# The first x rows loaded as two partition halves from two queues, and two small gate loads moved to GpSimd's queue

## The chip, the cores and the metric

The kernel runs on one core of a Trainium2 chip. The core has a matrix engine (TensorE, PE in the profile), VectorE (DVE), ScalarE (ACT), GpSimd (POOL), SyncE (SP, which here only issues DMAs) and 16 DMA engines that all queues share. Times are microseconds of device time for one execution; lower is better.

## The reference

The kernel mixes two spectral filters of the same input with a gate per row:

```python
def filt(x, w_r, w_i):                       # x: (1, 2048, 1024) bf16
    X = rfft2(x.astype(float32), axes=(-2, -1))
    X = X * (w_r + 1j * w_i)                  # w: (2048, 513)
    return irfft2(X, s=(2048, 1024), axes=(-2, -1)).astype(bfloat16)

g = sigmoid((A_x * gate_w).sum(-1, keepdims=True))   # gate_w: (1024,)
out = g * filt(A_x, A_w_r, A_w_i) + (1 - g) * filt(A_x, B_w_r, B_w_i)
```

## The kernel before

The Fourier transforms are done as matrix products with constant matrices. x is laid out as 64 x 2 groups on 128 partitions, with 16 "rows" j of 1024 elements in each partition (`x` is a view of the tile `XR`); the host has reordered the columns, so that sums and differences of column blocks give the even and odd frequencies.

Stage f1 multiplies each row j by the small matrix `F1` (tile `f` in the profile): 16 matmuls of 64 x 128 by 256 for one row, eight on partitions 0 to 63 and eight on 64 to 127 by turns (line 293); or, for rows that were folded beforehand, 16 matmuls of half the width (line 284). `xfold` (lines 267 and 268) is that fold: a sum and a difference on VectorE. Two halves of PSUM are then evicted to `y`, one by ScalarE and one by VectorE (helper `evac`, lines 250 and 252). Then follow f2 (line 347, products with `FD`), f3 (366, with `WF`), the product with the filter weights `cmul` (387), the way back i1 (414, with `WI`), a write of the result to DRAM scratch `sc` and its fetch in another order, and i2, i3 and the last sums.

The order of the work on each engine is written out by hand in the string `ORDER`, and every engine works through its instructions in that order. It begins `r0:AV V3 r1:AV r2:AV f3:AV r4:AV`: f1 of row 0, the fold of row 3 on VectorE, f1 of rows 1 and 2, f1 of the folded row 3, f1 of row 4. TensorE is kept busy from the start by eight matmuls on a zeroed tile `warm` (line 168). PSUM has eight banks; every stage takes two.

Loads. ScalarE's queue issues `F1` (line 170), `gws` (172, the gate vector, 128 partitions of 8 bf16) and `sg` (174, 128 partitions of one float). SP's queue issues x (line 180): rows 0 and 1 one by one (256 KB each), then pairs of rows (512 KB each), then rows 14 and 15 one by one; behind them `FD`, `WF`, the filter weights and the rest in one long stream. The framework gives the loads of SP and ScalarE eight completion semaphores in turn, so that the issue of one load waits until the load eight places before it has landed. GpSimd clears `gwz` (line 232) and later copies single columns of the weights (341) and issues the small copy `zt` (319).

VectorE turns `gws` into `gwz` with seven small instructions (lines 238 to 246) that stand ahead of all its evictions in its order. `gwz` is read at about 26 us, when the gate's sums are made (line 313); `sg` is read by the sigmoid (line 332) at about 40 us.

Of the kernel before, what the change touches and what calls it, by code (L numbers as in the profile page):

```python
# [141 lines left out]
def gated_mix(ctx, tc, x_in, we_in, wo_in, gw_in, out):  # L142
    nc = tc.nc
    cn = make_constants()
    dr = {n: nc.inline_tensor(a, name=f"cst_{n.lower()}").ap() for n, a in cn.items()}
# [23 lines left out]
    F1 = const.tile([P, 192], BF16, name="f1")  # L169
    nc.scalar.dma_start(F1[:], dr["F1"])  # L170
    gws = const.tile([P, 8], BF16, name="gws")
    nc.scalar.dma_start(gws[:], gw_in)
    sg = const.tile([P, 1], F32, name="sg")
    nc.scalar.dma_start(sg[:], dr["SG"])

    XR = big.tile([P, 16 * 1024], BF16, name="xr")
    RO = big.tile([P, 16 * 1024], BF16, name="ro")
    x = XR[:].rearrange("p (j d) -> p j d", j=16)
    for j0, n in ((0, 1), (1, 1)) + tuple((j, 2) for j in range(2, 14, 2)) + ((14, 1), (15, 1)):
        nc.sync.dma_start(x[:, j0:j0 + n, :], x_in[j0 // 2, :, j0 % 2:j0 % 2 + n, :])  # L180
    FD = const.tile([P, 2, 2, 2, 256], BF16, name="fd")
    IG = const.tile([P, 2, 4, 256], BF16, name="ig")
    WF = const.tile([P, NT, 3, 64], BF16, name="wf")
# [400 lines left out]
```

## Time and profile before

| | |
|---|---|
| median of 3 runs | 112.07 us (111.82 to 112.93) |
| the profiled execution | 112.45 us, of which the span of the core's instructions is 110.7 us |
| busy, share of the span | PE 92%, DVE 84%, ACT 83%, POOL 6% |
| HBM read, written | 24.23 MB, 12.58 MB |
| f1 of row 0 starts on PE | 4.71 us |
| f1 of row 2 starts on PE | 8.01 us, after 0.27 us of waiting for x |
| gate chain on DVE | 5.03 to 5.89 us |

Times inside an execution count from the start of the span. A timeline line gives start, duration, engine, source line, operation, tile written <- tiles read, count, and in brackets the idle time before it and what ended it. A line of the chain of waits gives start, duration and what the time went to. In the table by stretches the columns are the stretch, its length, busy time and number of instructions of PE, PE weight loads, DVE, ACT and POOL, the granted TensorE clock, the DMA engines' busy share and GB/s. A line of the DMA issues gives tile <- source, queue, operation, count, KB of each, and the median us from issue to landing.

### The profile page before, as it was taken

To read this page: it belongs to the slowest core of one execution; us is meant where nothing else is said; L and a number is where in the kernel's file an instruction comes from. 1 tells how busy PE (TensorE), PEld (TensorE's weight loads), DVE (VectorE), ACT (ScalarE), POOL (GpSimd) and SP (SyncE) were. 2 spreads that over 40 slices of the span, in tenths; PEclk is the share of its full clock that TensorE was granted. 3 is DMA by queue.
4 is the path that set the end of the run, shared out by engine and by line. 5 is a ranking of instruction groups with operands and counts; after the bars stand their busy time and mean duration, and the time that the engine had idled before them with its cause. 6 is when DMAs were issued, how large, how long until landed. Compare 5 with 4: busy or idle time off the path is not lost.

```text
span 110.7 us, 3975 instructions
## 1 busy us (share of the span) xinstructions
PE 101.7 (92%) x1669; PEld 65.7 (59%) x1672; DVE 93.4 (84%) x140; ACT 92.3 (83%) x179; POOL 6.7 (6%) x14
## 2 busy tenths in 40 slices
PE   5999997999999999999999999999999979999720
PEld 2369996765656565655555655455697866664400
DVE  0149987897859999999999999999989998678970
ACT  2346786698988999999999998999899998999730
POOL 1000000240520025000000000000000000000000
PEclk9999999999999999999999999999999999999997
DMA  3899999999999999979554999999997999995594
GB/s 111 208 342 418 407 410 405 415 421 390 407 410 397 400 394 392 402 282 294 196 190 136 278 282 403 395 381 354 374 314 206 367 349 394 419 412 235 240 378 191
DMA packets 17650, 37.07 MB, mean 335 GB/s; under 512 B 1884, under 2 KB 10208, under 8 KB 17632
## 3 DMA queue, kind: packets, MB, share of 16 engines
q1 hardware_dynamic: 17168, 36.76, 90.1%
q8 instruction: 13, 0.21, 0.8%
q10 hardware_dynamic: 432, 0.05, 0.3%
q14 instruction: 5, 0.04, 0.1%
q0 software_dynamic: 32, 0.00, 0.0%
HBM read 24.23 MB, written 12.58 MB: 333 GB/s over the span
## 4 chain that ended last, share of the span: by engine, by line
PE 66%; DMA 16%; DVE 6%; ACT 4%; issue 3%; SPq 1%; DVEq 0%; ACTq 0%
PE pt L414 27%; PE pt L347 12%; PE pt L366 6%; DMA ro<-sc 6%; DMA xr<-in_x_dram 6%; PE pt L296 4%; PE pt L293 4%; DMA sc<-rl 4%; PE pt L477 4%; PE pt L444 2%; DVE ot L508 2%; PE pt L459 2%; PE pt L313 2%; ACT V L250 1%; PE pt L284 1%
## 5 line engine op out<-in xcount | busy, mean ns | idle before, releaser
L414 PE MATMUL pt<-p,wi 64*64 64x512 bf16 x512 | 32.6, 379 | 0.1
L250 ACT CAST rl<-pt 128x512 bf16<-128x512 f32 x42 | 24.9, 660 | 1.9 <-PE pt L414 1.6
L387 DVE TENSOR_TENSOR p<-X,ro 128x4096 bf16<-128x4096 bf16 x11 | 25.2, 2295 | 1.2 <-ACT X L250 0.9
L414 PEld LDWEIGHTS <-wi 64*64 64x64 bf16 x512 | 13.3, 106 | 10.4 <-issue 1.5
L250 ACT CAST X<-pt 128x512 bf16<-128x512 f32 x29 | 16.7, 649 | 1.8 <-PE pt L366 1.6
L250 ACT CAST T<-pt 128x512 bf16<-128x512 f32 x30 | 17.3, 671 | 0.0
L347 PE MATMUL pt<-fd,y 128*128 128x256 bf16 x128 | 16.6, 274 | 0.0
L250 ACT CAST V<-pt 128x512 bf16<-128x512 f32 x30 | 16.5, 624 | 0.1
L252 DVE CAST rl<-pt 128x512 bf16<-128x512 f32 x22 | 14.7, 686 | 1.5 <-PE pt L414 1.4
L250 ACT CAST y<-pt 128x512 bf16<-128x512 f32 x17 | 9.7, 606 | 6.6 <-PE pt L293 5.3
L347 PEld LDWEIGHTS <-y 128*128 128x128 bf16 x128 | 11.3, 98 | 5.7 <-issue 4.3
L508 DVE TENSOR_TENSOR ot<-wo,od 128x1024 bf16<-128x1024 bf16 (+1 forms) x18 | 10.9, 631 | 1.3 <-DMA ro<-sc 0.8
L459 PE MATMUL pt<-ig,V 128*128 128x256 bf16 x88 | 11.6, 273 | 0.2
L252 DVE CAST y<-pt 128x512 bf16<-128x512 f32 x15 | 9.9, 686 | 1.4 <-PE pt L293 0.8
L366 PE MATMUL pt<-T,wf 64*64 64x512 bf16 (+2 forms) x192 | 9.8, 306 | 0.0
L387 DVE TENSOR_TENSOR p<-X,wo 128x4096 bf16<-128x4096 bf16 x4 | 9.1, 2284 | 0.0
L459 PEld LDWEIGHTS <-V 128*128 128x128 bf16 x88 | 7.6, 98 | 2.1 <-ACT V L250 1.0
L250 ACT CAST cs<-pt 128x512 bf16<-128x512 f32 x14 | 8.5, 654 | 0.0
L293 PE MATMUL pt<-f,xr 64*128 64x256 bf16 x112 | 7.9, 297 | 0.3 <-DMA xr<-in_x_dram 0.3
L366 PEld LDWEIGHTS <-wf 64*64 64x64 bf16 x192 | 5.3, 106 | 4.4 <-issue 0.4
L293 PEld LDWEIGHTS <-xr 64*128 64x128 bf16 x112 | 5.7, 104 | 2.5 <-issue 0.8
L250 ACT CAST od<-pt 128x512 bf16<-128x512 f32 x10 | 6.0, 624 | 1.4 <-PE pt L477 1.2
(51 smaller groups left out, 101.9 us busy)
## 6 DMA issues: line engine op xcount, KB each, us to landing
sc<-rl SPq DMA_DIRECT2D x16, 512.0 KB, 5.5
xr<-sc SPq DMA_DIRECT2D x8, 512.0 KB, 6.2
ro<-sc SPq DMA_DIRECT2D x8, 512.0 KB, 8.1
ro<-in_we_dram SPq DMA_DIRECT2D x7, 516.0 KB, 8.6
out_dram<-ot SPq DMA_DIRECT2D x7, 512.0 KB, 3.4
xr<-in_x_dram SPq DMA_DIRECT2D x6, 512.0 KB, 8.1
wo<-in_wo_dram SPq DMA_DIRECT2D x4, 512.0 KB, 7.5
ro<-in_wo_dram SPq DMA_DIRECT2D x4, 512.0 KB, 8.5
```

The lines of the kernel that those rows point to most:

```text
L250: nc.scalar.copy(out=out, in_=in_)
L252: nc.vector.tensor_copy(out=out, in_=in_)
L293: nc.tensor.matmul(pv[h][:, :, c, :, :].rearrange("p a e k -> p e a k"), lhsT=xs(j0, h, q), rhs=fs(h, 0, *st), start=(q == 0), stop=(q == 3))
L296: nc.tensor.matmul(pv[h][:, a, c, :, :], lhsT=xs(items[a][0], h, q), rhs=fs(h, items[a][1] * st[1], st[0]), start=(q == 0), stop=(q == 3))
L313: nc.tensor.matmul(ps[32 * j:32 * j + 32, :], lhsT=gwz[:, k, :], rhs=yf[:, 512 * j:512 * j + 512], start=(k == 0), stop=(k == 7))
L347: nc.tensor.matmul(ps[tt][:, e * 256:e * 256 + 256], lhsT=y[par][:, c, e, t].rearrange("p b s k -> p (b s k)"), rhs=FD[:, par, c, e, :], s ...
L366: nc.tensor.matmul(ps[tt][ho, dst:dst + ln], lhsT=WF[hp(j), 2 * u + tt, w, :], rhs=T[hp(j), tt, src:src + ln], start=(k == 0), stop=(k == 2))
L387: nc.vector.tensor_tensor(po, xo, wo, ALU.mult)
L414: nc.tensor.matmul(ps[tt][hp(j), :], lhsT=WI[hin, 2 * u + tt, w, :], rhs=p[hin, q, tt, a::2, o:o + 256], start=(k == 0), stop=(k == 3))
L459: nc.tensor.matmul(po, lhsT=V[:, s, 2 * r + c, :], rhs=IG[:, par, 2 * r + c, :], start=(c == 0), stop=(c == 1))
L477: nc.tensor.matmul(ps[s][:].rearrange("p (a d) -> p a d", a=2), lhsT=V[:, s, 2 * r + c, :], rhs=rhs, start=(r + c == 0), stop=(r + c == 2))
L508: nc.vector.tensor_tensor(o4[:, k, h] if not isinstance(od, list) else o4[:, k.start, h], x, y_, op)
```

## The change

Rows 0 to 3 (three loads: row 0, row 1, rows 2 and 3) are each loaded as two DMAs: partitions 0 to 63 from SP's queue, partitions 64 to 127 from ScalarE's queue. All later x loads stay whole on SP's queue. `gws` and `sg` are issued from GpSimd's queue instead of ScalarE's. On each engine the order of the other instructions is the same as before: SP still issues ten x loads, ScalarE issues F1 and the three halves ahead of its table load and first activation, and GpSimd issues gws and sg ahead of the clear of `gwz`. Line numbers after this place are two higher than before.

```diff
     F1 = const.tile([P, 192], BF16, name="f1")
     nc.scalar.dma_start(F1[:], dr["F1"])
     gws = const.tile([P, 8], BF16, name="gws")
-    nc.scalar.dma_start(gws[:], gw_in)
+    nc.gpsimd.dma_start(gws[:], gw_in)
     sg = const.tile([P, 1], F32, name="sg")
-    nc.scalar.dma_start(sg[:], dr["SG"])
+    nc.gpsimd.dma_start(sg[:], dr["SG"])
...
     for j0, n in ((0, 1), (1, 1)) + tuple((j, 2) for j in range(2, 14, 2)) + ((14, 1), (15, 1)):
-        nc.sync.dma_start(x[:, j0:j0 + n, :], x_in[j0 // 2, :, j0 % 2:j0 % 2 + n, :])
+
+        for q, h in ((nc.sync, slice(0, 64)), (nc.scalar, slice(64, 128))) if j0 < 4 else ((nc.sync, slice(0, 128)),):
+            q.dma_start(x[h, j0:j0 + n, :], x_in[j0 // 2, h, j0 % 2:j0 % 2 + n, :])
```

## The prediction

> **What bounds the kernel now.** I read the page first (TensorE busy for 92% of the span, VectorE 84%, ScalarE 83%), then the chain of waits in order of time, because the change touches the first microseconds only.
>
> ```profile
> 1.64 6.32 DMA xr<-in_x_dram
> ...
> 8.01 1.05 PE pt L293 x16
> 9.05 0.45 PE pt L284 x16
> 9.50 2.62 PE pt L293 x48
> ```
>
> The chain starts with the third x load (rows 2 and 3), which lands at 7.96 us and releases the f1 of row 2 (L293). From there the chain is nearly all TensorE as far as 78 us. What the change is worth is therefore what it does to TensorE's place at about 9 us. I next read the timeline of TensorE and of VectorE for that stretch.
>
> ```profile
> 1.18 3.60 PE L168 MATMUL pt<-warm 128*128 128x512 bf16 x8 [1.18 <-DVE warm L165]
> 4.71 3.03 PE L293 MATMUL pt<-f,xr 64*128 64x256 bf16 x32
> 8.01 1.05 PE L293 MATMUL pt<-f,xr 64*128 64x256 bf16 x16 [0.27 <-DMA xr<-in_x_dram]
> ```
> ```profile
> 5.03 0.17 DVE L238 TENSOR_SCALAR gh<-gws 128x8 f32<-128x8 bf16 x1 [3.91 <-DMA gws<-in_gw_dram]
> ...
> 5.73 0.16 DVE L246 TENSOR_TENSOR gwz<-gh 128x2 bf16<-128x2 f32 x1
> 6.66 0.69 DVE L252 CAST y<-pt 128x512 bf16<-128x512 f32 x1 [0.77 <-PE pt L293]
> 7.98 0.43 DVE L267 TENSOR_TENSOR xf<-xr 128x512 bf16<-128x512 bf16 x1 [0.63 <-DMA xr<-in_x_dram]
> 8.32 0.42 DVE L268 TENSOR_TENSOR xf<-xr 128x512 bf16<-128x512 bf16 x1
> ```
>
> TensorE waits only 0.27 us for rows 2 and 3. VectorE works in program order: the gate chain (7 instructions, 5.03 to 5.89), the eviction of row 0, the fold of row 3, and only then can f3 (L284, first matmul 8.89) start. Last, the stretches of the DMA traffic and the DMA issues:
>
> ```profile
> 2.00:3.00 1.00, 1.00 (x4) 0.44 (x3) 0.00 (x0) 0.88 (x1) 0.00 (x0) 1.00 0.97 347
> 3.00:4.00 1.00, 1.00 (x4) 0.32 (x3) 0.00 (x0) 0.60 (x2) 0.00 (x0) 1.00 0.94 209
> 4.00:5.00 1.00, 1.00 (x6) 0.24 (x6) 0.00 (x0) 0.00 (x0) 0.00 (x0) 1.00 0.92 162
> 5.00:6.00 1.00, 1.00 (x14) 0.67 (x12) 0.79 (x7) 0.00 (x0) 0.00 (x0) 1.00 0.68 217
> ...
> 8.00:9.00 1.00, 0.99 (x20) 0.90 (x22) 1.00 (x3) 0.38 (x1) 0.00 (x0) 1.00 1.02 418
> ```
> ```profile
> f<-cst_f ACTq DMA_DIRECT2D x1, 48.0 KB, 2.7
> gws<-in_gw_dram ACTq DMA_DIRECT2D x1, 2.0 KB, 3.9
> sg<-cst_sg ACTq DMA_DIRECT2D x1, 0.5 KB, 6.6
> ...
> zt<-zs POOLq DMA_DIRECT2D x1, 4.0 KB, 5.6
> ```
>
> The last column of the stretches is GB/s. The rate falls from 347 to 162 and returns to 418 only after 8 us, just while gws (landing at 5.0) and sg (1.63 + 6.6 = 8.2) trickle in. Issue and landing of the x loads tell the same: row 0 at 3.7, row 1 at 4.8, rows 2-3 at 7.96, rows 4-5 at 2.10 + 7.1 = 9.2, rows 6-7 at 10.5. From 7.96 on 512 KB take 1.25 us; between row 1 and rows 2-3 they took 3.2 us. The two tiny loads go with some 1.9 us of lost transfer.
>
> **The change, part by part.**
>
> *ScalarE's queue.* It issues four loads instead of three, at 0.36 to 0.49 us each: 0.5 us more, so the table load and its activation (1.28 and 0.20 us) end near 4.1. Its first eviction was at 6.63, so 2.5 us of slack hide this. Without that slack it would cost its 0.5 us.
>
> *SP's queue.* Ten issues as before. In before, SP stood 1.9 us waiting for sg before it could issue the last x load (a DMA waits for the one eight places before it). That wait goes. It is worth nothing: the transfers ran at 381 to 418 GB/s while SP waited, so the queue had work. The same holds for all later loads, which keep their relative order; if the stream runs up to a microsecond earlier, no TensorE wait of the chain between 9 and 79 us is for a load from the inputs.
>
> *Row 0 and TensorE's start.* TensorE needs both halves and F1. The second half now stands behind F1 in ScalarE's queue, and SP meanwhile moves row 1's first half and part of row 2-3. Best case it lands as before, 3.7; worst, as row 1 did, 4.8, plus the 0.4 us that ScalarE's issue lies behind SP's: 5.2. The warm-up matmuls cover it until 4.78. I take 4.7: nothing, with up to 0.4 us as the upper end.
>
> *Rows 2-3.* Loads that stood in the two queues at the same time have landed together by their number of rows, whatever the rows' size: F1 and row 0 (128 rows each) at 3.4 and 3.7, gws and row 1 at 5.0 and 4.8, sg and rows 2-3 at 8.2 and 7.96. If that is the rule, SP's 64 + 64 + 64 + 128 rows to the end of rows 4-5 run beside ScalarE's 128 (F1) + 64 + 64 + 64, and the second half of rows 2-3 ends with rows 4-5. The lower bound is the same 1.6 MB without tiny packets: begun at about 1.9, at 390 GB/s (between the 347 and 418 above), 6.0 us. The upper is today's landing of rows 4-5, 9.2. The tiny loads still exist, and part of their packets falls into this stretch: I take 8.2, near the row for rows 2-3 and two thirds of the way to the upper end. That is 0.2 us later than now; the bounds are -0.27 us (TensorE is busy until 7.74 anyway) and +1.2 us.
>
> *gws on GpSimd's queue.* The only row of that queue is zt: 0.77 us of issue, 5.6 us to landing. On ScalarE's queue gws took 3.9. GpSimd is free at 0.72. Bounds: 0.72 + 3.9 = 4.6 and 0.72 + 5.6 + 2.4 = 8.7, where 2.4 is what 128 tiny rows took beside a full queue (gws landed 1.6 us after F1 and sg 3.2 us after gws; the mean). Nearest is zt's own 5.6, and I add a third of the 2.4, 0.8, for twice its 64 rows and a second busy queue: landing 7.1. From there on VectorE's order gives: chain 0.86, gap 0.04, eviction 0.69, gap 0.03, fold to first f3 matmul 0.91, together 2.5 us. f3 starts at 9.6 instead of 8.89, so +0.7 us. Up to a landing of 6.4 it costs nothing; at 8.7 it costs 2.3. The delay of rows 2-3 lies under the same wait (f3 would start at 9.1 by it), so the larger counts. VectorE is then busy with one gap of 0.13 us until 16.4, TensorE without one until 18.46, and neither has room to make it up.
>
> *The rest of GpSimd.* The gwz clear (0.31 us) stands behind both issues and ends near 0.72 + 2 x 0.77 + 0.31 = 2.6; it is needed by the fourth instruction of the gate chain, after gws. sg is read at 40 us. Nothing for both.
>
> *Sum.* 0.7 us for the gate chain, 0 for all else. The profiled execution took 112.45 us with a span of 110.7 (1.75 around it); it lies 0.38 above the median of the runs, 112.07. So 113.15 for an execution like that one, 112.8 against the median. Under 1.1 us, 1%, a difference can hardly be told from none here; the forecast is inside that.
>
> **The rivals.**
>
> *A. gws comes much later.* GpSimd's first DMA of the kernel adds most of the 2.4 us: landing 8.1 to 8.7, +1.7 to +2.3 us, time 113.8 to 114.4. It decides from a landing of 7.5 on (+1.1). For: zt's 5.6, which had few packets. Against: zt was issued while VectorE ran a 2.3 us product (27.90 to 30.21), and GpSimd's next instruction beside it took 0.54 us where the one after it took 0.25; at 0.7 us VectorE is idle, so zt's row may be too slow a guide. The Trainium skill (SBUF — State Buffer, Who interferes with whom) says that such a product, with two inputs in SBUF, holds up only GpSimd instructions that read SBUF; by that rule, zt's 5.6 would not come from the product. No run here shows it. Chance 0.24.
>
> *B. The halves move slowly.* Two loads of 64 partitions each don't reach the rate of one over 128, or the tiny packets all fall into the stretch again: rows 2-3's second half lands with rows 4-5 at 9.2 or later. At half of 418 GB/s the 1.0 MB of rows 0 to 3 alone take 5.0 us, to 6.9, and half of the 1.9 us lost to the tiny loads, with part of rows 4-5 (512 KB, 1.25 us) between, make 9.1. TensorE starts row 2 at 9.2, +1.2 us, 113.3. For: equal numbers of rows in the two queues. Against: no row of before shows a half load; the one load over 64 partitions, zt, says nothing of rates. The Trainium skill (SBUF — State Buffer, "Can I just issue two DMAs to hit both halves?") speaks for this: two concurrent loads, at partition 0 and at partition 64, gave it only 6% over a single one, and it wants one load over all 128. No run here shows halves yet. Chance 0.18.
>
> *C. TensorE's full rate comes later.* The matmuls of L293 that start between 4.7 and 6.9 follow each other by about 0.10 us (22 of them), those after 9.5 by 0.055 (48 in 2.62 us). If row 0 is late enough to break the unbroken work since 1.18, the step to the full rate may come later; each 2 us at the low rate cost 0.9 us. With a step 2.7 us late: +1.2, 113.3. Nothing in this trace shows such a break. Chance 0.06.
>
> *D. It does what it says.* gws lands by 6.2 and rows 2-3 by 7.7: the 0.27 us wait goes, 111.8. For: the halves are moved at 390 GB/s if the tiny packets come late. Against: then gws is late too. Chance 0.12.
>
> **How the numbers follow.** Forecast 0.35, A 0.24, B 0.18, C 0.06, D 0.12; 0.05 stay for a gain over 1% that I can't derive, since 0.27 us is all that TensorE waits for these loads. Faster 0.05; within 1% 0.35 + 0.12 = 0.47; slower 0.24 + 0.18 + 0.06 = 0.48. The range goes from just under D, 111.7, into A, 114.2; the forecast's own is 112.1 to 113.1.
>
> **What would show it.** gws's issue on GpSimd's queue and its landing (7.1); the VectorE gate chain starting there; f3's first matmul (9.6); rows 2-3's second half (8.2); the GB/s between 3 and 6 us, which should rise if the tiny loads were the cause. Wrong if TensorE's first unbroken stretch starts before 7.9 or after 9.2, or if a wait elsewhere than in the first 10 us changes by over 0.5 us.

## The result, and the profile after

The changed kernel is slower: a ratio of 1.0129 to the kernel before (95% interval 1.0100 to 1.0157), 20 runs of each, medians 114.0 and 112.91 us. The ratio leaves out executions over 1.5% above the fastest of their kernel (7 of 20 before, 1 of 20 after); over all of them the medians differ by 1.09 us, 0.97%. The profiled execution took 113.27 us, its span 111.5. The load that TensorE waits for is now the second half of rows 2 and 3, on ScalarE's queue. First the chain of waits of the changed kernel, then its TensorE timeline and its VectorE timeline:

```profile
2.43 6.40 DMA xr<-in_x_dram
```
```profile
4.70 2.36 PE L295 MATMUL pt<-f,xr 64*128 64x256 bf16 x33
8.88 1.04 PE L295 MATMUL pt<-f,xr 64*128 64x256 bf16 x15 [1.81 <-DMA xr<-in_x_dram]
```
```profile
4.70 0.17 DVE L240 TENSOR_SCALAR gh<-gws 128x8 f32<-128x8 bf16 x1 [3.58 <-DMA gws<-in_gw_dram]
...
6.16 0.69 DVE L254 CAST y<-pt 128x512 bf16<-128x512 f32 x1 [0.60 <-PE pt L295]
8.92 0.42 DVE L269 TENSOR_TENSOR xf<-xr 128x512 bf16<-128x512 bf16 x1 [2.08 <-DMA xr<-in_x_dram]
```

The load is issued at 2.43 and lands at 8.83, where the whole load of before landed at 7.96. TensorE waits 1.81 us instead of 0.27 and starts row 2 at 8.88 instead of 8.01. (The start tells more than the wait: in before_again TensorE waited 0.79 us, more than the 0.1 to 0.5 that was expected of it, because rows 0 and 1 were done earlier, and still started row 2 at 8.02.) The gate chain on VectorE starts earlier than before, 4.70 against 5.03: gws came in good time. The fold of row 3 waits for the x load, not for the gate. The DMA issues and the stretches (the last column is GB/s):

```profile
xr<-in_x_dram ACTq DMA_DIRECT2D x1, 256.0 KB, 6.4
...
gws<-in_gw_dram POOLq DMA_DIRECT2D x1, 2.0 KB, 3.4
sg<-cst_sg POOLq DMA_DIRECT2D x1, 0.5 KB, 3.3
```
```profile
5.00:6.00 1.00, 1.00 (x18) 0.81 (x16) 0.52 (x6) 0.00 (x0) 0.00 (x0) 1.00 1.21 217
6.00:7.00 1.00, 1.00 (x19) 0.69 (x15) 0.69 (x1) 0.60 (x2) 0.00 (x0) 1.00 0.84 233
7.00:8.00 1.00, 0.07 (x1) 0.00 (x0) 0.00 (x0) 0.58 (x1) 0.00 (x0) 1.00 0.98 274
8.00:9.00 1.00, 0.12 (x3) 0.12 (x5) 0.08 (x1) 0.00 (x0) 0.00 (x0) 1.00 1.02 356
```

gws and sg both land by 5.3, and yet the rate stays under 280 GB/s until 8 us: worse than before (340 and 381 from 6 to 8). Between 7.1 and 8.9 us TensorE does nothing.

To separate the change from what varies anyway, I split the span at two marks: the first matmul of f2 (L347, L349 in the changed kernel) and the end of i1 (L414, L416). Each row is one profiled execution.

| kernel | profiled, us | rows 2-3 complete | f2 starts | f2 to end of i1 | end of i1 to end of span |
|---|---|---|---|---|---|
| before | 112.45 | 7.96 | 17.43 | 60.95 | 32.3 |
| before_again | 113.72 | 7.97 | 17.44 | 60.95 | 33.6 |
| after | 113.27 | 8.83 | 18.56 | 60.95 | 32.0 |
| after_again | 114.31 | 8.45 | 18.36 | 60.95 | 33.2 |

The middle is the same to a hundredth; what is lost before f2 is lost for good. The change costs 1.12 and 0.92 us there, about 0.9% of the time. The last stretch varies by over 1 us in either kernel, mostly by how long TensorE waits for the fetch of `sc` (before_again and after_again, the waits after 80 us):

```profile
PE pt L444 <- DMA ro<-sc: 1.8, 2, 1.3
```
```profile
PE pt L446 <- DMA ro<-sc: 0.9, 2, 0.6
```

after had no such wait, before 0.6 us. So the start of f2 is the sharper measure of this change; whole times that differ by some 0.5% may differ by this wait alone. What is over 0.9% in the ratio of 1.0129 isn't shown to come from the change.

In the changed kernel's two profiles, row 2 starts 0.87 and 0.49 us late. The rest (0.25 and 0.43) comes from 15.3 us on, where TensorE waits for rows 12 and 13. In after:

```profile
PEld L298 <- DMA xr<-in_x_dram: 0.2, 1, 0.2
```

That load landed at 15.65 and 15.36, some 2.5 us behind the one ahead of it, in place of 1.24 before (14.22). A 16 KB instruction fetch of 0.98 us begins at 13.3 to 13.6 us in both. Before has one of 0.95 us at 12.79 and no such gap, and the cause stays open.

### The profile page after: what moved, and what is told of

Its sections match the earlier page's. It is cut to its first block, busy times and chain, and to the rows that moved or that the text cites. A ratio compares the mean times of both kernels' runs of the same rounds, so it can differ in the third digit from the quotient of the medians.

```text
span 111.5 us, 3983 instructions
## 1 busy us (share of the span) xinstructions
PE 101.2 (91%) x1672; PEld 65.6 (59%) x1672; DVE 93.2 (84%) x140; ACT 92.1 (83%) x179; POOL 5.9 (5%) x16
## 4 chain that ended last, share of the span: by engine, by line
PE 73%; ACT 6%; DVE 6%; DMA 6%; issue 3%; ACTq 1%; DVEq 0%
PE pt L416 27%; PE pt L349 12%; PE pt L461 8%; PE pt L368 6%; DMA xr<-in_x_dram 6%; PE pt L446 5%; PE pt L298 4%; PE pt L295 4%; PE pt L479 3%; ACT V L252 3%; DVE ot L510 2%; ACT cs L252 2%; PE pt L315 2%; PE pt L286 1%; DVE p L389 1%
## 5 line engine op out<-in xcount | busy, mean ns | idle before, releaser
L416 PE MATMUL pt<-p,wi 64*64 64x512 bf16 x512 | 32.6, 379 | 0.0
L416 PEld LDWEIGHTS <-wi 64*64 64x64 bf16 x512 | 13.3, 106 | 10.4 <-issue 1.5
L252 ACT CAST V<-pt 128x512 bf16<-128x512 f32 x30 | 17.4, 682 | 0.1
L349 PE MATMUL pt<-fd,y 128*128 128x256 bf16 x128 | 16.6, 274 | 0.0
L349 PEld LDWEIGHTS <-y 128*128 128x128 bf16 x128 | 11.3, 98 | 5.7 <-issue 4.3
L295 PE MATMUL pt<-f,xr 64*128 64x256 bf16 x112 | 7.4, 278 | 1.8 <-DMA xr<-in_x_dram 1.8
L252 ACT CAST cs<-pt 128x512 bf16<-128x512 f32 x14 | 9.0, 713 | 0.0
L252 ACT CAST od<-pt 128x512 bf16<-128x512 f32 x10 | 6.5, 741 | 0.9 <-PE pt L479 0.9
```

The lines of the kernel that those rows point to most:

```text
L252: nc.scalar.copy(out=out, in_=in_)
L295: nc.tensor.matmul(pv[h][:, :, c, :, :].rearrange("p a e k -> p e a k"), lhsT=xs(j0, h, q), rhs=fs(h, 0, *st), start=(q == 0), stop=(q == 3))
L349: nc.tensor.matmul(ps[tt][:, e * 256:e * 256 + 256], lhsT=y[par][:, c, e, t].rearrange("p b s k -> p (b s k)"), rhs=FD[:, par, c, e, :], s ...
L416: nc.tensor.matmul(ps[tt][hp(j), :], lhsT=WI[hin, 2 * u + tt, w, :], rhs=p[hin, q, tt, a::2, o:o + 256], start=(k == 0), stop=(k == 3))
```

## The experiments

The stated theories: H, the halves cost; G, the two loads on GpSimd's queue cost. Under H, a half load is slow in itself (H1, later P), or it is the sharing of two queues (H2), or the number of issues (Q).

### One part alone

move_only has the two `nc.gpsimd.dma_start` lines of the change and loads x as before. halves_only has the halves and leaves `gws` and `sg` on `nc.scalar`.

> x is loaded whole from SP's queue as before; only gws and sg go to GpSimd's queue. Theory H (the halves are what costs: rows 2-3 arrive late because they are split over two queues): rows 2-3 land at 6.0 to 8.0, TensorE starts row 2 before 8.1, time 0.995 to 1.002 of before. Theory G (gws and sg on GpSimd's queue disturb the x loads): rows 2-3 land after 8.5 and the time is 1.008 or more of before. If the tiny packets on ScalarE's queue were what lowered the transfer rate between 3 and 6 us, that rate is over 300 GB/s here and rows 2-3 land before 7; if not, it stays near 200 GB/s and they land near 8.

> gws and sg stay on ScalarE's queue ahead of the second halves, the halves are as in the changed kernel. Theory H: as slow as the changed kernel or slower, since the second halves also stand behind two tiny loads: rows 2-3's second half lands at 9 to 10.5, time 1.01 to 1.03 of before. Theory G: rows 2-3 land near 8, time within 0.5% of before.

move_only: ratio 1.0011 (0.9968 to 1.0055), rows 2-3 at 8.15, f2 at 17.82. G falls as the cause of the loss: rows 2-3 land before 8.5, and the time can't be told from that of before. Nothing at all is more than the runs show, though. By the mark this one profile is 0.39 us late, 0.19 of it at row 2 (8.20), and late_even_odd below, which begins with the same loads, 0.27 (17.71). So part of the changed kernel's 0.92 to 1.12 us may go with the two moved loads. The rate between 3 and 7 us still falls, though gws's and sg's packets are out of ScalarE's queue; they land at 6.10 and 7.23, so they are still under way in that stretch:

```profile
3.00:4.00 1.00, 1.00 (x4) 0.32 (x3) 0.00 (x0) 0.00 (x0) 0.00 (x0) 1.00 0.88 225
...
5.00:6.00 1.00, 1.00 (x14) 0.67 (x12) 0.00 (x0) 0.00 (x0) 0.00 (x0) 1.00 0.85 213
6.00:7.00 1.00, 1.00 (x12) 0.70 (x10) 0.80 (x8) 0.37 (x1) 0.00 (x0) 1.00 0.85 283
```

halves_only: ratio 1.0133 (1.0054 to 1.0212); its executions spread from 113.7 to 118.2, median 116.27, and the ratio rests on the three shortest (113.74, 114.06, 115.38). The profile is of a long one (117.05). In it the second half of row 0 landed at 7.00 and that of rows 2-3 at 10.46. TensorE stood 1.95 us in the middle of row 0, and fell back to its low rate at about 8.4 us, ahead of the next wait. Its timeline, the stretches (the granted clock is third from the right), and the matmuls of line 295 from 10.5 to 16 us (minimum, median, maximum in ns):

```profile
7.04 2.64 PE L295 MATMUL pt<-f,xr 64*128 64x256 bf16 x32 [1.95 <-DMA xr<-in_x_dram]
10.50 1.88 PE L295 MATMUL pt<-f,xr 64*128 64x256 bf16 x15 [0.82 <-DMA xr<-in_x_dram]
```
```profile
8.00:9.00 1.00, 0.94 (x14) 0.71 (x14) 0.69 (x1) 0.59 (x1) 0.00 (x0) 0.78 1.02 234
9.00:10.00 1.00, 0.68 (x8) 0.15 (x2) 0.00 (x0) 0.49 (x1) 0.00 (x0) 0.50 0.98 258
```
```profile
L295 PE MATMUL pt<-f,xr x50: 269/417/418, 10.5 to 15.9; 64*128 64x256 bf16 x50
```

Half of these took 417 ns or more, where 269 is the full rate. The clock stays at 0.50 until about 15.3 us. f2 starts at 22.25, 4.8 us late, and the three executions that the ratio rests on are only 1.1 to 2.7 us longer than the median of before beside them (112.66), so they can't have lost as much. The full rate is not late here, as the prediction's rival C had it, but lost again, and in another kernel: the changed kernel's two profiles have 1.00 throughout the stretches to 16 us. The Trainium skill (TensorE: Matmul & The Clock Gate, Part 1) says that the clock is halved after an idle window of about 3.4 us; the one wait ahead of the fall, 1.95 us, is shorter. The measurement decides: the clock fell here with no longer wait between the first matmul and the fall. What brought it down, no experiment tried.

### Where the loads stand, and in which shape

```diff
 # halves_one_queue: the second half on SP's queue too
-... (nc.scalar, slice(64, 128))) if j0 < 4
+... (nc.sync, slice(64, 128))) if j0 < 4
 # whole_two_queues: rows 0 to 3 whole, one load for each row
+q = nc.scalar if j0 in (1, 3) else nc.sync
+q.dma_start(x[:, j0:j0 + n, :], x_in[j0 // 2, :, j0 % 2:j0 % 2 + n, :])
 # even_odd: halves of even and odd partitions
+(nc.sync, slice(0, 128, 2)), (nc.scalar, slice(1, 128, 2))
 # halves_rows23: "if j0 == 2";  halves_rows01: "if j0 < 2"
 # single_rows: move_only with rows 2 and 3 as two whole loads from SP's queue
 # f1_on_gpsimd: the changed kernel with F1 issued by nc.gpsimd
 # even_odd_f1: even_odd with F1 issued by nc.gpsimd
 # late_halves, late_even_odd: move_only, rows 8-9 and 10-11 as halves, all from SP's queue
```

> Both halves of each load are issued from SP's queue, one after the other; gws and sg on GpSimd's queue. Theory H1 (half loads are slow in themselves, whichever queue): rows 2-3 land at 8.8 or later, time 1.01 or more of before. Theory H2 (the second halves are late because rows 4-5 on SP's queue share the engines with them): here rows 4-5 stand behind both halves, rows 2-3 land where move_only has them plus the 1.2 us of three more issues at most, time below 1.006 of before.

> Rows 0 to 3 are loaded whole (128 partitions), one load for each row: 0 and 2 from SP's queue, 1 and 3 from ScalarE's; gws and sg on GpSimd's queue. Theory H1 (half loads are slow in themselves): rows 2 and 3 land at 8 or before, time within 0.5% of before. Theory H2 (sharing with rows 4-5 makes ScalarE's last load late): row 3 lands with rows 4-5 near 9, but row 2 earlier, TensorE starts row 2 before 8 and waits for the folded row 3 (its first matmul after 9.5 instead of 8.9), time 1.005 to 1.012 of before.

> As the changed kernel, but the two halves are the even and the odd partitions instead of 0 to 63 and 64 to 127: the same loads, rows, bytes, queues and issues. Theory P (a half load over 64 neighbouring partitions runs at half the rate, since these are only half of the ways into the memory; halves_one_queue had 256 KB in 1.25 us where whole loads have 512 KB): even and odd partitions each reach all of them, rows 2-3 land by 8.0, TensorE waits less than 0.5 us for row 2, time 0.997 to 1.005 of before. Theory Q (twice the number of loads, with their issue times and the sharing of two queues, is what costs): rows 2-3 land at 8.8 as in the changed kernel, time 1.009 to 1.016 of before.

> Only rows 2 and 3 are loaded as halves 0 to 63 and 64 to 127 from the two queues; rows 0 and 1 stay whole on SP's queue, gws and sg on GpSimd's. ScalarE's queue has only F1 and the second half. Theory P: the second half lands early (5 to 6.5), beside rows 0 and 1, and the first half, then alone, takes 1.25 us instead of 0.6: rows 2-3 complete at 7.5 to 8.5, time 0.997 to 1.006 of before. Theory Q: two more issues and sharing only: the same or better, 7 to 8. If rows 2-3 land after 8.8 the cost of halves lies in rows 2-3 themselves, and not in the four halves of rows 0 and 1 that stand ahead of them in the changed kernel.

> All x whole from SP's queue, rows 2 and 3 as two loads of 256 KB instead of one of 512 KB; gws and sg on GpSimd's queue. TensorE needs only row 2 first. All theories: row 2 lands at 6 to 7, the wait for it (0.27 us before) goes, row 3 at 8.0 to 8.2 holds the fold and f3 (first matmul 9.0), so at most 0.2 us is gained: time 0.996 to 1.002 of before.

> The changed kernel itself, for a second profiled execution and its times beside the other three on one chip. Expected: 1.010 to 1.016 of before; TensorE waits 1.0 to 2.0 us for rows 2 and 3. If the wait is much the same and the time is 114.0 to 114.5 instead of the 113.3 of the first profiled execution, the rest of the difference lies elsewhere in the span, and the two profiles tell where.

> The changed kernel, with F1's load moved from the head of ScalarE's queue to the head of GpSimd's, so that the two halves of each load stand at the same place of their queues. Theory H2 (ScalarE's halves are late because F1's 128 rows stand ahead of them and rows 4-5 on SP's queue take their turns meanwhile): the second half of rows 2-3 lands within 0.7 us of the first and both by 7.8, TensorE's wait for row 2 falls under 0.6 us, TensorE's f2 of unit 0 starts before 18.2 (18.56 and 18.36 in the changed kernel's two profiles, 17.43 before), time 1.000 to 1.007 of before. Theory Q (twice as many issues, each longer, is what costs, whatever the order): rows 2-3 land at 8.3 or later, f2 at 18.2 or later, time 1.009 or more. F1 may itself be late (landing over 4.8): then the first matmul starts later by as much, and f2 by no more than 0.5 us.

> Rows 0 and 1 as halves from the two queues, rows 2 and 3 whole from SP's queue behind its two first halves; gws and sg on GpSimd's queue. Theory H2: rows 2-3 stand on SP's queue, ahead of rows 4-5, and land by 8.2; the second half of row 1 by 6.2; TensorE's f2 of unit 0 starts before 18.0, time 0.998 to 1.006 of before. Theory Q: the two longer issues at the head of each queue delay everything behind them by 0.4 us or more: rows 2-3 at 8.4 or later, f2 after 18.0, time 1.004 to 1.010.

> The kernel before, for a second profiled execution. Expected of all theories: f2 of unit 0 starts at 17.2 to 17.9, TensorE waits 0.1 to 0.5 us for row 2. It tells how far the stretch from the end of i1 to the end of the span (32.3 us in the first profile, 32.0 and 33.2 in the changed kernel's two) varies without any change.

| kernel | ratio (95% interval) | rows 2-3: first, second part | f2 starts |
|---|---|---|---|
| halves_one_queue | 1.0131 (1.0060 to 1.0202) | 7.15, 8.40 | 18.83 |
| whole_two_queues | 1.0051 (1.0008 to 1.0094) | 6.05, 8.67 (rows 2, 3) | 17.95 |
| even_odd | 1.0042 (1.0000 to 1.0083) | 6.29, 9.14 | 18.68 |
| halves_rows23 | 1.0045 (0.9993 to 1.0097) | 7.26, 6.84 | 17.77 |
| halves_rows01 | 0.9986 (0.9950 to 1.0023) | 6.83 (whole) | 17.28 |
| single_rows | 0.9994 (0.9926 to 1.0062) | 6.90, 7.52 (rows 2, 3) | 17.30 |
| after_again | 1.0146 (1.0041 to 1.0250) | 6.81, 8.45 | 18.36 |
| f1_on_gpsimd | 1.0108 (1.0055 to 1.0160) | 9.44, 9.12 | 18.90 |

(after_again, halves_one_queue and f1_on_gpsimd have four executions each, the others ten.) Few theories met all their numbers: halves_one_queue landed at 8.40 where H1 had 8.8, whole_two_queues started f3 at 9.18 where H2 had 9.5, even_odd met P's ratio but Q's landing, halves_rows23 was complete at 7.26, ahead of P's 7.5 and within Q's 7 to 8, and f1_on_gpsimd met all of Q's, which halves_rows01 (6.83, where Q had 8.4) speaks against.

Three things follow. First, the place in the two queues matters. Counting rows of loads from the head of each queue, some loads that stand at the same count land at nearly the same time: in whole_two_queues rows 1 and 2 (256 rows) at 6.23 and 6.05, row 3 and rows 4-5 (384) at 8.67 and 8.13; in halves_rows01 row 1's second half and rows 2-3 (256) at 6.37 and 6.83; in the changed kernel the second half of rows 2-3 and rows 4-5 (320) at 8.83 and 9.43. It is no rule, though. In the changed kernel itself the second half of row 1 (256) lands at 5.62, ahead of the first half of rows 2-3 (192) at 6.74; in halves_rows23 the second half of rows 2-3 (192) lands at 6.84, long after row 1 (256) at 4.76; in halves_only 448 rows are in at 7.00 in one queue and at 11.42 in the other. With rows 2-3 whole and on SP's queue ahead of rows 4-5, as in halves_rows01, TensorE does not wait for them at all:

```profile
4.70 3.53 PE L295 MATMUL pt<-f,xr 64*128 64x256 bf16 x47
```

Second, the place isn't the whole. f1_on_gpsimd gives both halves the same place, they do land together, and late, at 9.1 to 9.4, and halves_one_queue has no sharing and is as slow as the changed kernel. H2 alone falls. Third, the parts don't add: halves of rows 0 and 1 alone cost nothing, halves of rows 2 and 3 alone 0.3 us at f2, no more than move_only without any (with rows 2-3 complete at 7.26, but 0.58 us of waiting for rows 12 and 13), both 0.9 to 1.1. even_odd stayed unclear: rows 2-3 as late as in the changed kernel, f2 too, and yet a ratio lower by 0.9%. Its profile has a last stretch of 32.3 us and after_again's one of 33.2; how much of the 0.9% is that, the runs don't tell.

### The half load by itself

> gws and sg on GpSimd's queue, all x from SP's queue, whole, except rows 8-9 and 10-11, which are loaded as halves 0 to 63 and 64 to 127 one after the other (four loads of 256 KB). Theory P (a half load runs at half the rate): these four land 1.2 to 1.3 us apart, at 200 to 220 GB/s, and the loads behind them 2.5 us later than in move_only. Theory Q (a half load costs its issue only, when the queue is not crowded): they land 0.62 us apart, at over 400 GB/s as whole loads do, and the loads behind them are at most 0.5 us late.

> As late_halves, with even and odd partitions as the halves. Theory P in the form that 64 neighbouring partitions reach only half of the ways into the memory: 0.62 us apart, over 400 GB/s. Theory P in the form that only a load over all 128 partitions gives each DMA engine a way of its own: between the two, 0.8 to 1.3 us apart. Theory Q: 0.62 us apart, like late_halves.

Behind rows that stream at over 400 GB/s, the two shapes differ by a factor of two. late_halves first, then late_even_odd:

```profile
8.00:9.00 1.00, 1.00 (x24) 0.91 (x24) 1.00 (x3) 0.42 (x2) 0.00 (x0) 1.00 1.08 414
...
10.00:11.00 1.00, 1.00 (x24) 0.90 (x20) 0.77 (x2) 0.44 (x2) 0.00 (x0) 1.00 1.04 234
...
13.00:14.00 1.00, 0.74 (x21) 0.50 (x17) 1.00 (x2) 0.78 (x2) 0.00 (x0) 1.00 1.02 234
```
```profile
10.00:11.00 1.00, 1.00 (x22) 0.89 (x20) 1.00 (x3) 0.76 (x2) 0.00 (x0) 1.00 1.00 406
11.00:12.00 1.00, 1.00 (x22) 0.89 (x20) 1.00 (x3) 0.72 (x2) 0.00 (x0) 1.00 1.01 414
```

In late_halves the four loads land at 13.15, 14.33, 15.97 and 17.29, over 1.1 us apart for 256 KB; in late_even_odd at 11.21, 11.85, 12.47 and 13.10, 0.63 us apart. Single executions took 118.03 and 113.75 us. A load over partitions 0 to 63 or 64 to 127 moves at about half the rate of one over all 128; a load of as many rows over every other partition does not. P in its first form holds.

These four loads come from one queue. Whether it holds too where two halves come from two queues at once, the packets tell. A packet of 4 KB is one partition of a pair of rows. Its median time from 9 to 17 us was 291 ns in late_halves and 159 in late_even_odd. From 5 to 8 us, with loads of both queues under way, it was 244 and 256 ns in the changed kernel's two profiles and 247 in f1_on_gpsimd, but 159 in before, even_odd and even_odd_f1. So the slow halves are in the changed kernel itself, and two of them at once did not make up for it.

> even_odd with F1's load moved to the head of GpSimd's queue: halves that move at the full rate, at the same place of both queues. Theory T (two causes: the half rate of neighbouring partitions, and the second half's place behind F1 beside rows 4-5; either is enough to make rows 2-3 late): with both gone both halves of rows 2-3 land by 7.7, TensorE's wait for them is under 0.4 us, f2 of unit 0 starts before 18.0, time 0.997 to 1.005 of before. Theory U (a third cause, such as two crowded queues and twice the issues in the first 8 us): rows 2-3 at 8.5 or later as in the other three, f2 after 18.3, time 1.004 to 1.012.

even_odd_f1 has a ratio of 1.0028 (0.9956 to 1.0099); rows 2-3 land at 7.92 and 7.49, f2 starts at 18.16. Against f1_on_gpsimd (9.44, 9.12), which differs in the partitions only, the half rate costs 1.5 us of landing (one profiled execution of each). The stretch from 7 to 8 us in f1_on_gpsimd, then in even_odd_f1:

```profile
7.00:8.00 1.00, 0.69 (x14) 0.36 (x8) 0.51 (x1) 0.50 (x2) 0.00 (x0) 1.00 1.02 266
```
```profile
7.00:8.00 1.00, 0.75 (x14) 0.78 (x16) 0.96 (x6) 0.00 (x0) 0.00 (x0) 1.00 1.01 385
```

Against even_odd (9.14), which differs in F1's place, the place costs 1.2. Taking away one of the two left rows 2-3 later than before; with both gone they land no later than before. Theory T's numbers were met for the ratio and for the wait for rows 2-3, which is gone, but not for the landing (7.7) nor for f2 (18.0): row 1's first half came late (7.11), and TensorE waited 0.98 us for it. So the two causes account for the late rows 2-3, and not for the whole loss: at the mark this kernel is still 0.73 us behind before, and its ratio doesn't exclude as much.

## Why the prediction was wrong

The forecast was 112.8 us, 0.65% over the 112.07 that it started from, and a difference inside 1%. The measured ratio, 1.29% with an interval that begins at 1.00%, is twice that. At the mark the change costs 0.92 to 1.12 us against the forecast 0.7. That this is near is luck: VectorE's wait for gws, which was to cost the 0.7 us, did not come, and rows 2-3, whose delay was to be hidden under it, cost the most. The sign was right, the mechanism was not.

*The step that failed is gws on GpSimd's queue.* It was the whole of the sum, 0.7 us, from a landing at 7.1. gws landed at 4.67, 3.4 us after its issue at 1.23, not 6.4 after 0.72, and f3 never waited for it. The one row that I had, zt's 5.6 us, was no guide, and the lower bound, 3.9 us as on ScalarE's queue, was the near one. In move_only gws took longer (1.24 to 6.10) and was still under the 6.4 from which it would count. Rival A, built on the same row, fell with it.

*Rows 2-3 were under-sized.* I took 8.2 and +0.2 us, hidden below the gate chain. They landed at 8.83 and 8.45, row 2 started 0.87 and 0.49 late, and nothing hid it. This is rival B, given 0.18: the second half lands next to rows 4-5, with the halves moving slowly. Its landing of 9.2 did not come, and its price, +1.2 us, was near the 0.9 to 1.1 found at f2 in part by luck, since 0.25 and 0.43 us of these come from rows 12 and 13. The rule of equal numbers of rows, from which the 8.2 was bounded, does not hold in general, as the counts above show. The Trainium skill (SBUF — State Buffer, "Can I just issue two DMAs to hit both halves?") was right to speak against this change, and its section on the DMA port swizzle says why partitions 0 to 63, and 64 to 127, are the bad case: each reaches 8 of 16 ports. late_halves agrees (234 against 414 GB/s); the ports themselves no run shows. I should have weighed that rule higher than a row of another DMA.

*That the tiny loads lowered the rate is not shown.* I read the fall to 162 GB/s between 3 and 6 us as gws and sg trickling in. move_only, with 225, 304 and 213 GB/s in the same stretches, shows a fall without them in ScalarE's queue, and in the changed kernel both have landed by 5.3 while the rate is 233 and 274 from 6 to 8. No run leaves them out. What two things did at the same time was taken for a cause. The reading of 381 to 418 GB/s while SP waited for sg (6.26 to 8.22) left out the 340 from 6 to 7.

*SP's queue, "ten issues as before", was short of the truth.* The count is right, but an issue of 64 rows took 0.57 to 0.70 us where one of 128 rows had taken 0.38 to 0.43. The start is slower with it, 198 GB/s from 2 to 3 us against 347. In halves_rows01, with 180 there, it cost nothing.

*No TensorE wait behind 9 us for an input* held in before, and not in the changed kernel: rows 12 and 13 came late and cost the remaining 0.25 to 0.43 us. I had taken it for granted that the stream keeps its pace.

*Right were* TensorE's start at 4.70, ScalarE's extra issues and GpSimd's clear, which nothing waited for (ScalarE's first activation ended at 4.57, not 4.1, and its first eviction came at 6.12), and that what is lost in the first 9 us is not made up: f2 to the end of i1 took 60.95 us in all four profiles. Row 2 also started inside the 7.9 to 9.2 us that were to hold (8.88 and 8.50): that sign could not tell the wrong mechanism from the right one, and gws's landing could.

## What to carry to other kernels

If a load has to be split, don't split it into partitions 0 to 63 and 64 to 127: split it by rows of the free dimension, whole over 128 partitions, as single_rows does, or by every other partition. Keep a load that work is waiting for near the head of its queue and off a second one; counting the rows ahead of it in each queue is a rough guide at best, and several loads here did not keep to it. And measure such a change at a mark close to it (here the start of f2), since a later, unrelated wait can vary by as much as the whole effect.

## What the runs showed that I had not expected

- Issuing a DMA of 64 partitions took longer than one of 128 with the same row length: 0.57 us against 0.38 at the head of SP's queue. Rows 4-5, whole, right behind the halves, took 0.60 too.
- The rate falls to 156 to 300 GB/s somewhere between 3 and 7 us in these kernels, whatever the queues, and is about 400 or more from 9 to 10 us on in most. In halves_rows01 the fall is the shortest, 205 from 3 to 4 us and 324 and 338 from 4 to 6. It goes with a few long packets: in before and before_again six and eight packets of 4 KB that began between 3.9 and 4.6 us took over 1 us each, where the median is 159 ns; in halves_rows01 none of 4 KB took over 0.57. What held them up was not found.
- GpSimd's queue brought 128 rows of 16 bytes in 2.5 us (halves_one_queue, 1.24 to 3.77) to 5.2 us (whole_two_queues, 1.24 to 6.40), from issue to landing.
- TensorE, once at its full rate, can fall back: in the profile of halves_only a wait of 1.95 us was followed by some 1.4 us of work at 269 ns a matmul and then, from 8.6 us on, by matmuls at 417 ns until about 15 us.
